# Spectral filter and two MLPs in float32 on one core: eight instead of four early products of the second sequence's first stage, and a reordered last group

## The chip, the core and the metric

The kernel runs on one core of a Trainium2 chip. The metric is the device time of one execution in microseconds (us), the whole program from the first to the last instruction and what little lies around it. TensorE multiplies matrices into PSUM, ScalarE (ACT) and VectorE (DVE) evacuate PSUM and do the elementwise work, GpSimd (POOL) does a few elementwise steps out of SBUF and issues some loads, and SyncE (SP) issues most of the DMA transfers.

## The reference, cut to what matters

```python
# batch 2, seq 3008, dim 256; d_ff 2048
X = np.fft.rfft(x, axis=1)
Y = X * (filt_r + 1j * filt_i)[None]
x = np.fft.irfft(Y, n=3008, axis=1).reshape(6016, 256)
h = x @ w_in                                   # first network
x = np.where(h > 0, h, np.exp(np.minimum(h, 0)) - 1) @ w_out
h = x @ w2_in                                  # second network
out = (h * np.clip(h + 3, 0, 6) / 6) @ w2_out
```
The inputs and weights are float32, or float64 where setup yields that; the output is float32.

## The kernel before, in words

**The transform.** A length of 3008 is 47 x 64. A sequence goes through four matrix stages: a first stage over 47 (table `s1` or `s1t`), a second over 64 (`s2`), the filter, the inverse second stage (`i2`), and the inverse first stage (`i1`). The dim of 256 is two halves h of 128. For sequence 0 all of this is the **prologue**; for sequence 1 it is done beside the first network's units. A string `PROLOGUE` is the order of the prologue, written out by hand. Its steps, with h and an index behind the letter, are:

- T: four transposes of first-stage results `zt`, and their copy out of PSUM; A: a first-stage piece of the second half (matmuls with `s1t`, then a copy into `zt`).
- S: the second-stage matmul and `mult`, three VectorE multiplications (L192 twice, L193) with the filter tile; GpSimd adds their results (L195). F: GpSimd flips the sign of part of the next filter tile (`f_sign`, L128). I: the inverse second-stage matmul (L200), its evacuation and a write to DRAM (L207).
- V: four reloads of these writes (L211), which wait for all six writes of a half. O and o: the inverse first stage (L219) with evacuation on ScalarE or VectorE. X: split of a block of the result for the first network.
- x: load of a tile of sequence 1 (`x_load`, SP); b: split of half such a tile into two float32r parts (ScalarE rounds, L78; VectorE subtracts, L79); B: the product of the first stage of sequence 1 on it, three matmuls (L82 to L84), its evacuation and write. M: split of the table `s1`; m: its load.
- w: load of a float64 weight tile as raw words (`w_raw`); c and k: steps of its conversion to two float32r parts (L261 to L286; c for weight tile 0).

`LOADS` is the order of the first loads on SP's queue: four tiles of sequence 0 (half 0), then F (filter tile), W (weight tile), X (tile of sequence 0, half 1).

**The first network** runs in 192 units of 12 matmuls, each a block of 512 tokens times a weight tile of 128 of d_ff: six for `g1`, six for `g2`. Lists `pre[n]` and `post[n]` hold what else is done at unit n: conversions of weights, and sequence 1's transform from unit 48 on (`s1(h, i, t)` puts a first-stage product at unit t, with its load, split and evacuation around it).

**The second network** runs over six pairs of blocks p and eight pairs of weight tiles q, 48 groups, with Strassen-like sums: seven products `prod(p, q, m)` of three matmuls and eight second products. A group's blocks (0,0), (1,1), (1,0), (0,1) each go through an add, `relu`, `gate` and `part` (ScalarE rounds, VectorE subtracts), then `second`. The blocks (1,0) and (0,1) of a group are finished in the next one, where it is `old`. `beside` holds work for the next pair: loads, four GpSimd subtractions (`x_sums`) and seven operand splits (`x_part`).

All products in float32 accuracy are three float32r matmuls (`mm3`): high times low, low times high, high times high. Buffers come from rotating pools: `wpool` of sixteen 4 KB tiles a partition for converted weights, `p4` and `p2` of twenty tiles.

## Time and profile before

| | |
|---|---|
| times of three runs | 1125.74, 1136.16, 2869.24 us (median 1136.16) |
| the profiled execution | 1131.49 us, span 1129.7 us |
| mean granted TensorE clock | 0.993 |
| TensorE busy | 1110.8 us, 98% of the span |
| VectorE, ScalarE, GpSimd busy | 884.0, 793.5 and 150.5 us |
| DMA in the first 84 us | 282, 299 and 254 GB/s in three stretches of 28 us |

TensorE is busy nearly throughout, and the chain of work that ended last lies on it for 90% of the span. That share says nothing of the first 76 us, in which the engines hand each other short pieces, nor of the last 13. [...] In a row of the timeline the bracket at the end is the idle time before it and what ended it.

### The profile page before, as it was taken

Reading aid. Unit: us, or ns where it says so; the run is one execution under the profiler, and the core shown is the slowest. Engines: PE = TensorE matmul, PEld = TensorE weight load, DVE = VectorE, ACT = ScalarE, POOL = GpSimd, SP = SyncE. Lnnn points to the kernel's source line nnn. Section 1 sums busy time; section 2 is a strip of 40 time slices with the busy share of each in tenths; the row PEclk is TensorE's granted clock in tenths of the full one; section 3 lists DMA queues with packets and bytes.
Section 4 is the critical chain, followed back from the end, with each engine's and each line's share of the span. In section 5 each row is a group of like instructions: output and inputs, shape, how many; then the busy total and the mean of one; then the engine's idle time right before and its main releaser. Section 6 shows DMA issues by size and latency. Waiting matters only on the chain.

```text
span 1129.7 us, 14294 instructions
## 1 busy us (share of the span) xinstructions
PE 1110.8 (98%) x5068; PEld 919.7 (81%) x5068; DVE 884.0 (78%) x1376; ACT 793.5 (70%) x1406; POOL 150.5 (13%) x141
## 2 busy tenths in 40 slices
PE   8899999999999999999999999999999999999997
PEld 5588888788789888888889878878878878888996
DVE  6979999669983588888897677777777777777775
ACT  3477777877766777777777667767767767767664
POOL 3600000013330011111224110010010010000000
PEclk9989999999999999999999999999999999999999
DMA  9973100364523123323427900200200200200100
GB/s 284 300 254 125 38 5 1 112 182 161 173 86 84 54 75 112 112 94 112 149 90 256 323 1 1 75 1 1 75 1 1 75 1 1 70 1 1 38 1 33
DMA packets 56472, 100.50 MB, mean 89 GB/s; under 512 B 4816, under 2 KB 33872, under 8 KB 56400
## 3 DMA queue, kind: packets, MB, share of 16 engines
q1 hardware_dynamic: 51968, 86.65, 23.2%
q0 software_dynamic: 3456, 12.58, 3.2%
q8 instruction: 40, 0.66, 0.2%
q10 hardware_dynamic: 976, 0.34, 0.1%
q14 instruction: 32, 0.26, 0.1%
HBM read 65.22 MB, written 34.34 MB: 88 GB/s over the span
## 4 chain that ended last, share of the span: by engine, by line
PE 90%; DVE 4%; DMA 2%; ACT 1%; issue 1%; POOL 0%; SPq 0%; ACTq 0%; DVEq 0%; POOLq 0%
PE ps L82 29%; PE ps L83 29%; PE ps L84 29%; PE ps L219 3%; DVE t L79 1%; DMA t<-in_fq 1%; DMA t<-in_xp 1%; DVE t L500 1%; PE ps L200 1%; DVE t L192 1%; DMA id<-in_ident 0%; DVE t L389 0%; DVE t L193 0%; DVE t L492 0%; POOL t L195 0%
## 5 line engine op out<-in xcount | busy, mean ns | idle before, releaser
L82 PE MATMUL ps<-t,w 128*128 128x512 f32 (+1 forms) x1296 | 502.5, 388 | 2.8 <-DVE t L79 2.6
L83 PE MATMUL ps<-t,w 128*128 128x512 f32 (+1 forms) x1296 | 500.0, 386 | 0.0
L84 PE MATMUL ps<-t,w 128*128 128x512 f32 (+1 forms) x1296 | 499.8, 386 | 0.0
L79 DVE TENSOR_TENSOR t<-t,t 128x512 fp32r<-128x512 f32 (+2 forms) x490 | 350.7, 726 | 80.7 <-ACT t L78 75.2
L78 ACT ACTIVATE t<-t 128x512 fp32r<-128x512 f32 (+2 forms) x490 | 293.6, 614 | 97.4 <-DVE t L500 72.8
L82 PEld LDWEIGHTS ps<-t,w 128*128 128x128 f32 x1296 | 243.7, 188 | 53.1 <-DVE t L79 3.5
L84 PEld LDWEIGHTS ps<-t,w 128*128 128x128 f32 x1296 | 243.7, 188 | 45.7
L83 PEld LDWEIGHTS ps<-t,w 128*128 128x128 f32 x1296 | 243.8, 188 | 45.2
L389 DVE SCALAR_TENSOR_TENSOR t<-t,ps 128x512 f32<-128x512 f32 (+1 forms) x192 | 129.2, 673 | 89.6 <-ACT t L388 88.3
L387 ACT ACTIVATE t<-ps 128x512 f32<-128x512 f32 (+1 forms) x192 | 112.2, 584 | 95.9 <-PE ps L84 95.7
L500 DVE SCALAR_TENSOR_TENSOR t<-t,t 128x512 f32<-128x512 f32 (+1 forms) x144 | 102.5, 712 | 33.9 <-ACT t L496 33.5
L496 ACT ACTIVATE t<-t,three 128x512 f32<-128x512 f32 (+1 forms) x144 | 97.6, 709 | 44.3 <-DVE t L492 43.0
L388 ACT ACTIVATE t<-t 128x512 f32<-128x512 f32 (+1 forms) x192 | 119.7, 623 | 6.1
L486 ACT ACTIVATE t<-ps 128x512 f32<-128x512 f32 (+1 forms) x144 | 83.3, 578 | 24.4 <-PE ps L84 23.2
L492 DVE TENSOR_TENSOR t<-ps,t 128x512 f32<-128x512 f32 (+1 forms) x144 | 94.2, 672 | 4.8 <-PE ps L84 2.3
L435 POOL TENSOR_TENSOR t<-t,t 128x512 f32<-128x512 f32 (+1 forms) x18 | 25.4, 1411 | 287.2 <-PE ps L84 281.4
L128 POOL TENSOR_TENSOR t<-t,sg 128x512 f32<-128x512 f32 x24 | 30.4, 1271 | 195.1 <-DMA t<-in_fq 195.1
L82 PE MATMUL ps<-t,t 128*128 128x512 f32 (+1 forms) x120 | 46.8, 390 | 3.4 <-ACT t L486 3.4
L84 PE MATMUL ps<-t,t 128*128 128x512 f32 (+1 forms) x120 | 46.3, 386 | 0.0
L83 PE MATMUL ps<-t,t 128*128 128x512 f32 (+1 forms) x120 | 46.3, 386 | 0.0
L195 POOL TENSOR_TENSOR t<-t,t 128x512 f32<-128x512 f32 x24 | 34.1, 1420 | 74.3 <-DVE t L193 56.5
L500 DVE SCALAR_TENSOR_TENSOR t<-t,ps 128x512 f32<-128x512 f32 (+1 forms) x48 | 32.3, 674 | 11.9 <-ACT t L496 11.9
(79 smaller groups left out, 854.4 us busy)
## 6 DMA issues: line engine op xcount, KB each, us to landing
t<-in_fq SPq DMA_DIRECT2D x24, 512.0 KB, 6.5
scrw<-t SPq DMA_DIRECT2D x16, 512.0 KB, 2.8
w<-scrw POOLq DMA_DIRECT2D x16, 512.0 KB, 7.5
t<-in_xp SPq DMA_DIRECT2D x16, 384.0 KB, 5.6
scr<-t SPq DMA_DIRECT2D x24, 256.0 KB, 2.5
t<-scr SPq DMA_DIRECT2D x16, 384.0 KB, 5.0
scrx<-t SPq DMA_DIRECT2D x10, 512.0 KB, 3.1
t<-scrx SPq DMA_DIRECT2D x10, 512.0 KB, 5.3
```

What stands on the lines that cost most here:

```text
L78: nc.scalar.activation(hi, src, AF.Copy)
L79: nc.vector.tensor_tensor(out=lo, in0=src, in1=_f32(hi), op=ALU.subtract)
L82: nc.tensor.matmul(acc, wh, xl, start=start, stop=False, skip_group_check=more)
L83: nc.tensor.matmul(acc, wl, xh, start=False, stop=False, skip_group_check=more)
L84: nc.tensor.matmul(acc, wh, xh, start=False, stop=stop, skip_group_check=more)
L387: nc.scalar.activation(r[:, :n], acc[:, :n], AF.Relu, scale=-1.0)
L388: nc.scalar.activation(r[:, :n], r[:, :n], AF.Exp, scale=-1.0)
L389: nc.vector.scalar_tensor_tensor(out=r[:, :n], in0=r[:, :n], scalar=-1.0, in1=acc[:, :n], op0=ALU.add, op1=ALU.max)
L486: nc.scalar.activation(t[:, : self.n], bank_[:, : self.n], AF.Copy)
L492: nc.vector.tensor_tensor(out=self.h[key][:, :n], in0=bank_[:, :n], in1=u[:, :n], op=ALU.add)
L496: nc.scalar.activation(self.g[key][:, : self.n], self.h[key][:, : self.n], AF.Relu, bias=three)
L500: nc.vector.scalar_tensor_tensor(out=r[:, :n], in0=r[:, :n], scalar=6.0, in1=self.h.pop(key)[:, :n], op0=ALU.min, op1=ALU.mult)
```

## The change

- The prologue's tail does eight instead of four first-stage products of sequence 1 (B00 to B07, all of half 0); `s1(0, 4..7)` at units 48 to 51 goes. All four x tiles are loaded in the prologue; the last two lie in two tiles of `wpool`.
- `LOADS` no longer holds W1 and W2, which the steps w00 and w01 load again anyway; W0 goes behind F10, F03 ahead of the X tiles.
- The conversion steps of weight tile 0 and the split of `s1` go behind the multiplications S10 to S15; `s1` is loaded at the start with the other tables.
- The zero-fill of x tiles beyond row 96 goes, and the first stage contracts 96 rows.
- In a group of the second network `old.part((0, 1))` goes behind the product 6 and its copy `u2`. The work for the next pair is spread: one GpSimd subtraction in each of the groups 1 to 4 instead of two in groups 2 and 3, loads one group earlier, splits from group 2.
- In the last group the two halves of `part` (`high`, `low`) are placed singly, ahead of the add that waits for product 3 where they can be, and the last evacuation is halved between ScalarE and VectorE.

```diff
     def x_load(b, h, q):
-        xin[b, h, q] = t4([P, 8, P])
-        if b == 0:
-            nc.vector.memset(xin[b, h, q][KP:], 0.0)
+
+        xin[b, h, q] = wpool.tile([P, 8, P], F32, tag="w", name=name("w")) if (b, h) == (1, 0) and q > 1 else t4([P, 8, P])
...
-    def out_evac(p, k):
+    def out_evac(p, k, last=False):
...
+            m = n if d == 0 else n // 2 if last else 0
+            if m:
+                nc.scalar.activation(t[:, :m], o[:, :m], AF.Copy, scale=1.0 / 6.0)
+            if m < n:
+                nc.vector.tensor_scalar_mul(t[:, m:n], o[:, m:n], 1.0 / 6.0)
...
+        def high(self, key):
+            g, gh = self.g[key], t2([P, 512], F32R)
+            nc.scalar.activation(gh[:, : self.n], g[:, : self.n], AF.Copy)
+            self.g[key] = g, gh
+
+        def low(self, key):
+            (g, gh), gl, n = self.g[key], t2([P, 512], F32R), self.n
+            nc.vector.tensor_tensor(out=gl[:, :n], in0=g[:, :n], in1=_f32(gh[:, :n]), op=ALU.subtract)
             self.g[key] = gh, gl
...
         g.relu((0, 0))
-        if old:
-            old.part((0, 1))
         g.gate((0, 0))
         prod(p, q, 6, a, False)
         u2 = g.copy(a)
+        if old:
+            old.part((0, 1))
...
-        A12 A13 c01 A14 I03 F01 c01 A15 A16 I04 c02 T10 T11 F01 I05 V00 T12 S10 x00 x01 T13 S11 T14 S12 M00 F01
-        T15 S13 I10 F01 S14 c01 I11 S15 I12 w00 O00 I13 b00 O01 c01 b01 I14 o02 I15 b02 c01 V10 w01 c01 b03 O03 X00
-        o04 X01 k02 O05 o06 X02 k02 B00 B01 B02 B03
+        A12 A13 A14 I03 F01 A15 A16 I04 T10 T11 F01 I05 c02 V00 T12 S10 x00 x01 x02 x03 T13 S11 T14 S12 F01
+        T15 S13 I10 F01 S14 I11 S15 I12 w00 O00 I13 c01 b00 O01 I14 c01 b01 o02 I15 M00 c01 b02 V10 w01 c01 b03 O03
+        X00 c01 o04 X01 k01 O05 B00 b04 o06 X02 b05 B01 B02 b06 k01 B03 B04 b07 k02 B05 B06 B07
...
-    for x in "F00 W0 F01 F02 X0 X1 X2 X3 F03 F04 W1 F05 F10 F11 F12 W2 F13 F14 F15".split():
+    for x in "F00 F01 F02 F03 X0 X1 X2 X3 F04 F05 F10 W0 F11 F12 F13 F14 F15".split():
...
-    for i in range(4, 8):
-        s1(0, i, T - 4 + i)
...
-            1: [(x2_load, 0), (x2_load, 1)], 2: [(x_sums, 0), (x_sums, 1)], 3: [(x_sums, 2), (x_sums, 3)],
-            4: [(x_part, 1), (x_part, 2)], 5: [(x_part, 6), (x_part, 5)], 6: [(x_part, 7), (x_part, 4)],
-            7: [(x_part, 3)],
+            0: [(x2_load, 0), (x2_load, 1)], 1: [(x_sums, 0)], 2: [(x_sums, 1), (x_part, 1)],
+            3: [(x_sums, 2), (x_part, 2)], 4: [(x_sums, 3), (x_part, 5)], 5: [(x_part, 6)],
+            6: [(x_part, 7), (x_part, 4)], 7: [(x_part, 3)],
...
         prod(5, NF // 2 - 1, 3, old.c, False)
+        old.high((1, 1))
+        old.gate((1, 0))
         old.add((0, 1), old.u2, old.c)
+        old.low((1, 1))
+        old.high((1, 0))
         old.relu((0, 1))
-        old.part((1, 1))
-        old.gate((1, 0))
+        old.low((1, 0))
         old.gate((0, 1))
-        old.part((0, 1))
-        old.part((1, 0))
-        old.second((0, 0))
-        old.second((1, 1))
-        old.second((0, 1))
-        out_evac(old.p, 1)
-        old.second((1, 0))
-        out_evac(old.p, 0)
+        old.high((0, 1))
+        old.low((0, 1))
+        for key in ((0, 0), (1, 1), (1, 0), (0, 1)):
+            old.second(key)
+            if key == (1, 0):
+                out_evac(old.p, 0)
+        out_evac(old.p, 1, True)
```

First place: VectorE in the prologue, from the second to last copy into `zt` to the first multiplication of the second half (S10). `raw_132` and `raw_150` are weight tile 0's raw words, `t_93` and `t_88` the copy of T11's transposes. Before:

```order
L75 COPY zt_328<-ps_365 128x5x4x24
L262 TENSOR_SCALAR t_81_373<-raw_132 128x512
L266 SCALAR_TENSOR_TENSOR t_81_373<-raw_132,t_81_373 128x512
L75 COPY zt_328<-ps_391 128x5x4x24
L268 SCALAR_TENSOR_TENSOR t_80_372<-t_80_372,t_81_373 128x512
L270 TENSOR_SCALAR t_81_373<-t_80_372 128x512
L75 COPY t_93_421<-ps_416 128x512
L192 TENSOR_TENSOR t_104_447<-ps_444,t_18_160 64x512 x2
```

and in the changed kernel:

```order
L75 COPY zt_314<-ps_351 128x5x4x24
L75 COPY zt_314<-ps_371 128x5x4x24
L75 COPY t_88_399<-ps_394 128x512
L261 TENSOR_SCALAR t_92_408<-raw_150 128x512
L265 SCALAR_TENSOR_TENSOR t_92_408<-raw_150,t_92_408 128x512
L191 TENSOR_TENSOR t_102_431<-ps_428,t_16_148 64x512 x2
```

The four conversion steps stood ahead of T11's copy, two of them ahead of the last `zt` copy; now two stand behind that copy, and the other two behind S15.

Second place: VectorE in the last stages of the prologue, from the split of the second block (X01) to the last conversion step there. `t_174` and `t_183` or `t_187` are blocks of the result, `raw_545` and `raw_528` weight tile 1, `w_441` and `w_443` the two x tiles in the weight pool. Before:

```order
L79 TENSOR_TENSOR t_174_643<-t_148_572,t_173_642 128x512
L262 TENSOR_SCALAR t_177_650<-raw_545 128x512
L266 SCALAR_TENSOR_TENSOR t_177_650<-raw_545,t_177_650 128x512
L75 COPY t_180_662<-ps_664 128x188
L79 TENSOR_TENSOR t_183_669<-t_155_593,t_182_668 128x512
L268 SCALAR_TENSOR_TENSOR t_176_649<-t_176_649,t_177_650 128x512
L270 TENSOR_SCALAR t_177_650<-t_176_649 128x512
```

and in the changed kernel:

```order
L79 TENSOR_TENSOR t_174_633<-t_148_556,t_173_632 128x512
L261 TENSOR_SCALAR t_177_640<-raw_528 128x512
L79 TENSOR_TENSOR t_184_660<-w_441,t_183_659 96x512
L75 COPY t_180_651<-ps_663 128x188
L79 TENSOR_TENSOR t_187_668<-t_154_575,t_186_667 128x512
L79 TENSOR_TENSOR t_189_672<-w_441,t_188_671 96x512
L79 TENSOR_TENSOR t_194_688<-w_443,t_193_687 96x512
L265 SCALAR_TENSOR_TENSOR t_177_640<-raw_528,t_177_640 128x512
L79 TENSOR_TENSOR t_199_705<-w_443,t_198_704 96x512
L267 SCALAR_TENSOR_TENSOR t_176_639<-t_176_639,t_177_640 128x512
L269 TENSOR_SCALAR t_177_640<-t_176_639 128x512
```

Four subtractions for the added products (b04 to b07) have come in between, the last of them two steps ahead of the end.

Third place: ScalarE at the head of a group of the second network. The two copies out of one `ps` are those after product 1 and after product 6 (`u2`); the rows with `three` are the `relu` of (0,1) and (0,0), and the rounding of (0,1) reads the first of these. Before:

```order
L486 ACTIVATE t_1554_6636<-ps_6630 128x512
L78 ACTIVATE t_1556_6643<-t_1547_6615 128x512
L496 ACTIVATE t_1558_6647<-t_1550_6628,three 128x512
L496 ACTIVATE t_1559_6656<-t_1555_6641,three 128x512
L78 ACTIVATE t_1560_6658<-t_1558_6647 128x512
L486 ACTIVATE t_1562_6666<-ps_6630 128x512
L78 ACTIVATE t_1563_6671<-t_1559_6656 128x512
```

and in the changed kernel:

```order
L487 ACTIVATE t_1553_6625<-ps_6619 128x512
L78 ACTIVATE t_1555_6632<-t_1546_6604 128x512
L497 ACTIVATE t_1557_6636<-t_1549_6617,three 128x512
L497 ACTIVATE t_1558_6645<-t_1554_6630,three 128x512
L487 ACTIVATE t_1559_6651<-ps_6619 128x512
L78 ACTIVATE t_1560_6653<-t_1557_6636 128x512
L78 ACTIVATE t_1562_6660<-t_1558_6645 128x512
```

The copy `u2` has moved ahead of the rounding of (0,1), which reads what VectorE's gate writes.

## Rows read from the trace of the kernel before

**Rows 1.** Busy time by stretch, after the prologue: us, engines' busy (instructions), clock, DMA.

```profile
197.00:1129.70 932.70, 922.53 (x4174) 771.91 (x4172) 713.13 (x1099) 664.65 (x1176) 120.74 (x112) 1.00 0.23 77
```

**Rows 2.** Timeline of TensorE in the prologue: start, us, instruction, idle time before it.

```profile
38.01 1.06 PE L152 MATMUL ps<-id,zt 128*128 128x128 f32 x8 [2.54 <-DVE zt L75]
...
52.79 1.63 PE L200 MATMUL ps<-t,i 128*128 128x512 f32 x2 [1.42 <-POOL t L195]
...
54.21 2.29 PE L219 MATMUL ps<-i,t 96*128 96x94 f32 x10
...
69.22 7.28 PE L219 MATMUL ps<-i,t 96*128 96x94 f32 x64
```

**Rows 3.** Busy time by stretch, behind that wait; clock and DMA share near the end.

```profile
56.00:60.00 4.00, 4.00 (x15) 2.97 (x15) 2.55 (x4) 2.25 (x5) 1.58 (x1) 0.50 0.50 167
```

**Rows 4.** Second network: TensorE's wait in all, then timelines of GpSimd, VectorE, ScalarE.

```profile
PE ps L82 <- ACT t L486: 3.4, 5, 0.7
...
661.00 1.30 POOL L435 TENSOR_TENSOR t<-t 128x512 f32<-128x512 f32 x1 [8.94 <-ACT t L486]
662.26 1.74 POOL L435 TENSOR_TENSOR t<-t,t 128x512 f32<-128x512 f32 x1
...
661.64 1.20 DVE L79 TENSOR_TENSOR t<-t,t 128x512 fp32r<-128x512 f32 x1
662.77 1.77 DVE L500 SCALAR_TENSOR_TENSOR t<-t,t 128x512 f32<-128x512 f32 x1
...
665.85 0.68 DVE L500 SCALAR_TENSOR_TENSOR t<-t,t 128x512 f32<-128x512 f32 x1
...
664.58 0.63 ACT L78 ACTIVATE t<-t 128x512 fp32r<-128x512 f32 x1 [1.95 <-DVE t L500]
```

**Rows 5.** The tail: timelines of VectorE and TensorE, and busy time by stretch.

```profile
1117.10 0.62 DVE L492 TENSOR_TENSOR t<-ps,t 128x448 f32<-128x448 f32 x1 [1.08 <-PE ps L84]
...
1119.61 0.47 PE L82 MATMUL ps<-t,w 128*128 128x448 f32 x1 [1.33 <-DVE t L79]
...
1122.01 0.74 PE L82 MATMUL ps<-t,w 128*128 128x448 f32 x1 [0.89 <-DVE t L79]
...
1121.00:1125.00 4.00, 3.11 (x9) 2.69 (x9) 1.51 (x3) 1.30 (x3) 0.00 (x0) 0.58 0.00 0
```

**Rows 6.** Timeline of VectorE in the prologue, and busy time by stretch (VectorE's is third).

```profile
26.41 1.39 DVE L192 TENSOR_TENSOR t<-ps,t 64x512 f32<-64x512 f32 x2 [2.42 <-POOL t L128]
...
34.58 0.94 DVE L262 TENSOR_SCALAR t<-raw 128x512 uint32<-128x512 uint32 x1
35.56 1.41 DVE L266 SCALAR_TENSOR_TENSOR t<-raw,t 128x512 uint32<-128x512 uint32 x1
...
47.84 1.37 DVE L102 TENSOR_TENSOR s_l<-s,s_h 128x96 fp32r<-128x96 f32 x1
...
53.38 0.90 DVE L272 SCALAR_TENSOR_TENSOR t<-raw,t 128x512 f32<-128x512 uint32 x1
...
41.32:56.39 15.07, 13.35 (x51) 7.66 (x49) 14.72 (x22) 5.25 (x9) 8.75 (x7) 0.90 0.91 250
56.39:70.04 13.65, 13.65 (x69) 10.76 (x69) 9.50 (x18) 8.41 (x18) 1.58 (x1) 0.74 0.51 150
```

**Rows 7.** Timeline of TensorE in the main loop: two matmuls twelve apart.

```profile
92.26 0.39 PE L84 MATMUL ps<-t,w 128*128 128x512 f32 x1
...
94.98 0.39 PE L84 MATMUL ps<-t,w 128*128 128x512 f32 x1
```

**Rows 8.** Timelines of GpSimd and of SP's DMA issues in the prologue.

```profile
25.34 1.04 POOL L128 TENSOR_TENSOR t<-t,sg 128x512 f32<-128x512 f32 x1 [2.25 <-DMA t<-in_fq]
...
19.17 5.32 SPq L123 DMA_DIRECT2D t<-in_fq  x4
...
43.04 1.73 SPq L211 DMA_DIRECT2D t<-scr  x4
...
65.20 1.73 SPq L211 DMA_DIRECT2D t<-scr  x4
```

More of the change, by code (lines that the diff above doesn't have):

```diff
@@ L139, in s1t @@
             nc.tensor.matmul(
-                acc[:, (j - j0) * KP : (j - j0 + 1) * KP], xin[b, h, j // 8][:, j % 8, :],
-                mats["s1t"], start=True, stop=True,
+                acc[:, (j - j0) * KP : (j - j0 + 1) * KP], xin[b, h, j // 8][:KP, j % 8, :],
+                mats["s1t"][:KP], start=True, stop=True,
             )
@@ L472, in out_evac @@
             o, t = outs.pop((p, k, d)), t2([P, 512])
-            if d == 0:
-                nc.scalar.activation(t[:, :n], o[:, :n], AF.Copy, scale=1.0 / 6.0)
-            else:
-                nc.vector.tensor_scalar_mul(t[:, :n], o[:, :n], 1.0 / 6.0)
+            m = n if d == 0 else n // 2 if last else 0
[3 more added lines that the diff above has]
+                nc.vector.tensor_scalar_mul(t[:, m:n], o[:, m:n], 1.0 / 6.0)
             nc.sync.dma_start(out[d * P : (d + 1) * P, t0 : t0 + n], t[:, :n])
@@ L508, in part @@
             self.g[key] = gh, gl
+        def high(self, key):
[5 more added lines that the diff above has]
+            nc.vector.tensor_tensor(out=gl[:, :n], in0=g[:, :n], in1=_f32(gh[:, :n]), op=ALU.subtract)
+            self.g[key] = gh, gl
         def second(self, key, d=(0, 1)):
@@ L606, in fft_conv_moe_moe2 @@
     PROLOGUE = """
-        T00 T01 T02 S00 T03 F01 S01 T04 F01 S02 T05 F01 S03 I00 F01 S04 I01 F01 m00 A10 A11 S05 I02 F01
-        A12 A13 c01 A14 I03 F01 c01 A15 A16 I04 c02 T10 T11 F01 I05 V00 T12 S10 x00 x01 T13 S11 T14 S12 M00 F01
-        T15 S13 I10 F01 S14 c01 I11 S15 I12 w00 O00 I13 b00 O01 c01 b01 I14 o02 I15 b02 c01 V10 w01 c01 b03 O03 X00
-        o04 X01 k02 O05 o06 X02 k02 B00 B01 B02 B03
+        T00 T01 T02 S00 T03 F01 S01 T04 F01 S02 T05 F01 S03 I00 F01 S04 I01 F01 A10 A11 S05 I02 F01
+        A12 A13 A14 I03 F01 A15 A16 I04 T10 T11 F01 I05 c02 V00 T12 S10 x00 x01 x02 x03 T13 S11 T14 S12 F01
+        T15 S13 I10 F01 S14 I11 S15 I12 w00 O00 I13 c01 b00 O01 I14 c01 b01 o02 I15 M00 c01 b02 V10 w01 c01 b03 O03
+        X00 c01 o04 X01 k01 O05 B00 b04 o06 X02 b05 B01 B02 b06 k01 B03 B04 b07 k02 B05 B06 B07
         O10 o11 X10 O12 X11 k03 O13 X12 O14 O15 O16
@@ L704, in fft_conv_moe_moe2 @@
     with tc.manual_schedule():
-        for key, src in (("s1t", cs1t), ("id", ident), ("sg", sg), ("s2", cs2), ("i2", ci2), ("i1", ci1)):
+        for key, src in (("s1t", cs1t), ("id", ident), ("sg", sg), ("s2", cs2), ("i2", ci2), ("i1", ci1), ("s1", cs1)):
             load_mat(key, src)
@@ L768, in fft_conv_moe_moe2 @@
                 s1_evac(1, h, g)
-            elif what == "m":
-                load_mat("s1", cs1)
             elif what == "M":
```

## The prediction

> **What bounds the kernel now.** I began with the page's totals and then asked where TensorE idles: after the prologue it is busy for 922.53 of 932.70 us [rows 1]. So there an edit is worth either the matmul time that it takes off TensorE or the holes that it closes, about 10 us of them in all. Next I listed TensorE's waits by cause and looked up each in the timeline. [...] In the second network five holes stand behind ScalarE's copy L486, 3.4 us together [rows 4]. At the end two holes of 1.33 and 0.89 us stand behind the last group's subtractions, and the clock is 0.58 on the mean from 1121 to 1125 [rows 5]. The prologue itself is a chain on VectorE, which works for 14.72 of the 15.07 us from 41.32 to 56.39 [rows 6].
>
> **The sum is made against the profiled execution:** 1131.49 us, of which the span is 1129.7. It lies between the two ordinary runs shown (1125.74 and 1136.16, mean 1130.95). The third, 2869.24, is no ordinary run, so the median of the three is simply the slower ordinary one.
>
> **Term A, the four products that leave the main loop.** Each is three matmuls of 512 columns, so twelve. Two matmuls twelve apart start at 92.26 and 94.98 [rows 7]: 2.72 us. They stood at units 48 to 51, in the stretch where TensorE hardly idles [rows 1], so all of it is on the path: -2.7.
>
> **Term B, the holes in the second network.** At 661.00 and 662.26 two GpSimd subtractions run back to back, and VectorE's gate L500 beside the second takes 1.77 us instead of 0.68. ScalarE idles 1.95 us for that gate, with its rounding L78 of block (0,1) at the head of its queue; the copy L486 that TensorE needs for product 7 stands behind it, and TensorE loses 0.7 [rows 4]. The change takes the cause away twice: the copy goes ahead of that rounding (third place of the order), and a group holds one GpSimd subtraction, never two. The five holes go: -3.4. What is late next in a group is the rounding and subtraction of (0,1), about 0.6 + 0.7 us, which TensorE wants only after products 5 and 7 and two pairs of second products: 18 matmuls, 4.1 us by [rows 7]. So nothing follows. [...]
>
> **Term C, the tail.** In the last group TensorE finishes six second products after product 3, then waits 1.33 and later 0.89 us [rows 5], because every rounding and subtraction follows the add that waits for product 3 (1117.10 to 1117.72). In the new order the rounding of (1,1) and the gate of (1,0) go ahead of that add. At 0.6 us a piece, from the add's end: subtraction (1,1) until 1118.4, (1,0) until 1118.9, last gate 1119.5, rounding 1120.1, subtraction (0,1) 1120.7. TensorE's blocks of six matmuls of 448 columns (1.2 us, by columns from [rows 7]) want them at 1118.2, 1119.4 and 1120.6, so 0.3 of the 2.2 us of holes stay. With the holes I expect the low clock to stay away. [...] The last evacuation, a VectorE instruction as long as that add (0.62 us), is cut into halves on two engines: -0.3. Sum -(1.9 + 1.6 + 0.3) = -3.8; the bound is -2.2 if the clock falls all the same.
>
> **Term D, the prologue,** along VectorE.
> - The multiplication S03 begins at 26.41 after 2.42 us of waiting [rows 6] for the filter tile F03, whose sign GpSimd makes once the load is there, at 25.34 [rows 8]. F03 is now loaded ahead of the four X tiles, and F04 takes the queue place that F03 had, since W0 went behind. So S04 can follow one GpSimd instruction after 25.34, at 26.4 instead of 28.6: -2.2 for all behind it.
> - The word steps L262 and L266, 0.94 + 1.41 us, stood ahead of the last zt copy [rows 6] and go behind T11's copy (first place of the order). The transposes at 38.01 then start at about 33.5. S10 has those two steps in front of it, but no longer the next two and no idle time: about 38.4 instead of 41.32, -2.9.
> - Of the 15.07 us from there to the end of S15, the split of s1 (0.2 + 1.37) and L272 (0.90) leave [rows 6]: 12.6. S15 ends at about 51.0, -5.4.
> - Then the bill. From 56.39 to 70.04 VectorE works 9.50 us and idles 4.1 [rows 6]. Behind S15 now come also L268 and L270 (1.1), the split (about 1.2), L272 (0.7) and four subtractions for the added products (0.65 each): 15.1 without a hole, so 66.1 instead of 70.04 (second place of the order). The last subtraction for a product stands two steps ahead of that, at 65.2; as ScalarE's roundings ahead of it are queued with evacuations, I take 66.0.
> - TensorE does not bind here: from about 54 it has 34 small rows (3.9 us by the 64 in 7.28 [rows 2]) and 24 matmuls (5.5 us). B07 ends at 66.7 and O10 starts there instead of 69.22: -2.5. The 64 rows behind it take 7.1 us as before (their last one's end overlaps the next), and the main loop starts at 73.8 instead of 76.3.
> - O10 also needs the reload V1, issued at 65.20 [rows 8] and there within 4.0 us, since O10 started at 69.22 without a wait. The transfers that begin with the reload V0 at 43.04 fill the DMA engines until they are half idle in 56 to 60 [rows 3, 8]. They begin 4 us earlier now and hold two x tiles of 384 KB more. Four tiles of 512 KB were issued in 5.32 us with the queue full [rows 8], 1.33 each, so two of 384 KB are 2.0 to 2.7: they end at about 57, the last writes behind them at 58 to 59, and V1 is there by 63. That is 3 us of cover; if the -2.9 did not come, it would be gone.
> So D is -2.5; its bounds are -5.5 (ScalarE and VectorE keep pace with TensorE, B07 at 63.7) and +2.6 (the clock, first rival).
>
> **At nothing:** the eight zero-fills on VectorE, because what TensorE waits for next is the fourth x load and a later ScalarE copy; 96 instead of 128 rows contracted, since time goes by columns; the second loads of W1 and W2, whose places in the queue are in D; the early load of s1, behind six other small ones; the two x tiles in two of sixteen weight buffers, read out by 67, long before the fifteenth weight tile wants one.
>
> Sum: -2.7 - 3.4 - 3.8 - 2.5 = -12.4, so 1131.49 - 12.4 = **1119 us**.
>
> **Rivals.** *The clock falls again, later.* In my working TensorE waits for the operands of B04 to B07, 2.8 us of work in about 6. Before, the drop followed a hole of 1.42. If it drops again, it falls on the 64 rows of O1x and the first units: a spell of 10 us, as before, costs up to 5.1, and D turns from -2.5 to +2.6: 1124. For it: the same kind of hole, longer. Against: the wait of 2.54 at 38 brought no drop. [...] *The products only change place.* TensorE has no hole from 54 to 76, so one may say that eight products there cost what four in the loop cost, and D is -2.5 + 2.7, nothing: 1121.5. [...] *GpSimd's delay spreads.* Two delays, 1.20 - 0.68 and 1.77 - 0.68, are 1.6 us and cost TensorE 0.7, so 0.9 was free; a full subtraction of 1.30 [rows 4] would cost 0.4, in 20 groups 8 us, and B is +8 instead of -3.4: 1130. Against: the copy no longer stands behind the gate. *Slower:* VectorE's subtraction for (0,1) now waits for a rounding that waits for the copy after product 6, in 47 groups, with the subtraction of (0,0), the operand splits and the next add queued behind it. If TensorE then waits d in each group, the time is 1119 + 47 d: from d = 0.27 it is slower than before, and with a full subtraction of 0.69 it is 1151. Against: the 4.1 us of cover, and that the gate of (0,0) now goes ahead.
>
> **How the numbers follow.** Forecast 0.50, clock 0.23, products only moved 0.15, GpSimd 0.04, slower 0.02; 0.06 for a better case, in which the clock does not fall in the prologue or the tail (the ordinary runs lie 10.4 apart, twice the price of such a spell): 1125.74 - 12.4 = 1113. The range takes in that case, the first two rivals and, above 1124, half the spread of the runs: 1112 to 1129. Two per cent, about what a measurement of this kernel can tell from no change, is 23 us, twice my sum. So within 2%: 0.93; faster by more 0.05, where the better case is set against the slower ordinary run; slower by more 0.02.
>
> **What would show it.** A: twelve matmuls fewer in units 48 to 51. B: no wait of TensorE for the copy in the second network, though gates beside GpSimd are still long. C: TensorE's last 24 matmuls without a hole over 0.4 us, at full clock. D: the second half's transposes at 33 to 34, S15's end near 51, O10 near 66.7, the first unit near 73.8, the granted clock at 1.00 there. I would be wrong if the clock shows a spell behind B04, if O10 waits for V1, or if TensorE has a new short wait in each group.

## The result

The changed kernel is about 1% slower. It takes 1142.5 us (median of four runs, 1139.7 to 1145.2) against 1132.6 for the kernel before, a ratio of 1.0108 with a 95% interval of 1.0071 to 1.0146. One of the four runs of the kernel before took 2869.24 us and is left out of the ratio, which rests on the other three (1125.74 to 1136.16). The forecast was 1119, its range 1112 to 1129. The profiled execution took 1143.72 us, 1142.0 of it the span.

First I cut the span at events that both kernels have: TensorE's first product of the main loop, and the first and the last matmul that reads the sums of the weights (zt) in the second network. These are the three stretches between and behind them, first in the kernel before, then in the changed one (us, engines' busy time with instructions, granted clock as a share of full speed, DMA share, GB/s).

```profile
76.28:633.02 556.74, 555.25 (x2536) 464.23 (x2536) 456.20 (x717) 422.26 (x771) 91.80 (x89) 1.00 0.35 117
633.02:1071.10 438.08, 434.68 (x1918) 358.74 (x1916) 333.33 (x514) 303.07 (x515) 28.94 (x23) 1.00 0.09 32
1071.10:1129.71 58.61, 52.78 (x251) 47.81 (x249) 36.40 (x63) 33.30 (x61) 0.00 (x0) 0.96 0.05 16
```

```profile
100.84:655.25 554.41, 552.90 (x2525) 463.04 (x2524) 450.74 (x708) 417.26 (x759) 91.81 (x89) 1.00 0.33 110
655.25:1086.74 431.49, 431.49 (x1917) 359.63 (x1916) 335.40 (x514) 301.65 (x515) 28.57 (x23) 1.00 0.09 32
1086.74:1141.95 55.21, 51.10 (x251) 46.70 (x249) 35.97 (x63) 33.22 (x62) 0.00 (x0) 0.99 0.05 18
```

Each stretch got shorter: by 2.3, 6.6 and 3.4 us. In the second network TensorE is now busy for 431.49 of 431.49 us, and near the end, where [rows 5] show holes and the lower clock, a window of the changed kernel has neither:

```profile
1133.00:1137.00 4.00, 3.93 (x20) 3.32 (x19) 2.91 (x6) 2.28 (x4) 0.00 (x0) 1.00 0.01 4
```

All of the loss lies ahead of the main loop, which starts at 100.84 us instead of 76.28; the forecast was 73.8. These are the rows of TensorE there, which answer to [rows 2] (start, us, instruction, idle time before it), first the start of the kernel before, then the changed kernel:

```profile
5.32 3.87 PE L139 MATMUL ps<-s1t,t 128*128 128x96 f32 x32 [0.22 <-DVE t L118]
10.43 3.78 PE L139 MATMUL ps<-s1t,t 128*128 128x96 f32 x32 [1.24 <-DMA t<-in_xp]
14.88 1.50 PE L152 MATMUL ps<-id,zt 128*128 128x128 f32 x12 [0.67 <-ACT zt L73]
...
17.16 0.60 PE L152 MATMUL ps<-id,zt 128*128 128x128 f32 x4
```

```profile
5.30 13.97 PE L138 MATMUL ps<-s1t,t 96*128 96x96 f32 x64 [0.20 <-DMA s1t<-in_cs1t]
19.85 2.82 PE L151 MATMUL ps<-id,zt 128*128 128x128 f32 x12 [0.58 <-ACT zt L73]
...
24.17 0.62 PE L151 MATMUL ps<-id,zt 128*128 128x128 f32 x4
...
81.33 0.71 PE L82 MATMUL ps<-t,s_h 96*96 96x512 f32 x1 [10.58 <-DVE t L79]
...
85.94 0.74 PE L82 MATMUL ps<-t,s_h 96*96 96x512 f32 x1 [3.05 <-DVE t L79]
...
87.34 13.80 PE L218 MATMUL ps<-i,t 96*128 96x94 f32 x64
```

Three things are new. The 64 first rows (32 products: the trace counts a float32 matmul as two) take 13.97 us without a stop, where they took 3.87 and 3.78, so the first transposes start 5.0 us later; these still run at half speed (2.82 us for 1.50), and the next group starts 7.0 us later (24.17 for 17.16). TensorE waits 10.58 and 3.05 us for operands of the added products B06 and B07. Behind that the 64 rows that read the last reload take 13.80 us where they took 7.28 [rows 2]. The windows of the two idle times and of what follows show the clock, which answers to [rows 3]:

```profile
71.00:81.30 10.30, 0.00 (x0) 0.00 (x1) 0.81 (x2) 1.59 (x3) 0.00 (x0) 0.55 0.72 221
81.30:102.00 20.70, 17.62 (x73) 16.14 (x74) 8.43 (x15) 8.60 (x20) 0.00 (x0) 0.50 0.58 178
```

While TensorE stood idle for 10.30 us, the granted clock fell to its lower level (0.55 on the mean), and it stayed there until the main loop had begun (0.50 from 81.30 to 102.00 us). TensorE's wait is put down to VectorE's subtraction, but VectorE works 0.81 us in 10.30. So the next step is what VectorE waits for, and it is ScalarE: first ScalarE's waits for these writes (us in all, times, longest), then its timeline, then SyncE's DMA issues.

```profile
ACT t L168 <- DMA scr<-t: 16.9, 3, 10.7
...
68.07 0.59 ACT L168 ACTIVATE t<-ps 96x512 f32<-96x512 f32 x1
79.35 0.59 ACT L168 ACTIVATE t<-ps 96x512 f32<-96x512 f32 x1 [10.69 <-DMA scr<-t]
79.84 0.62 ACT L78 ACTIVATE t<-w 96x512 fp32r<-96x512 f32 x1
...
67.29 1.73 SPq L210 DMA_DIRECT2D t<-scr  x4
...
71.59 18.57 SPq L170 DMA_DIRECT2D scr<-t  x4
```

L168 evacuates an added product, and two of them fill one tile, which L170 writes to DRAM. The next pair's evacuation takes the slot of the tile that is being written, so it waits until that write has landed. The rounding L78 of the next operand is queued behind it on ScalarE; VectorE's subtraction needs that rounding, and TensorE needs the subtraction. The first write was issued at 71.59, behind the reload of the second half and four loads of weights, and took 7.7 us to land; the other three took about 3 us, and the evacuations that wait for them 3.1 us each.

### The profile page after: what moved, and what is told of

Same layout as the page of the kernel before. It is cut to its first block, busy times and chain, and to the rows that moved or that the text cites. A ratio compares the mean times of both kernels' runs of the same rounds, so it can differ in the third digit from the quotient of the medians.

```text
span 1142.0 us, 14236 instructions
## 1 busy us (share of the span) xinstructions
PE 1118.4 (98%) x5068; PEld 931.6 (82%) x5068; DVE 875.8 (77%) x1368; ACT 792.6 (69%) x1407; POOL 148.6 (13%) x141
## 4 chain that ended last, share of the span: by engine, by line
PE 91%; DMA 4%; DVE 2%; ACT 1%; issue 1%; POOL 1%; SPq 0%; ACTq 0%; POOLq 0%
PE ps L82 29%; PE ps L84 29%; PE ps L83 29%; PE ps L218 2%; DMA t<-in_fq 2%; DMA scr<-t 1%; DMA t<-in_xp 1%; DVE t L79 1%; PE ps L138 1%; PE ps L199 1%; POOL t L194 0%; DMA id<-in_ident 0%; DVE t L388 0%; PE ps L182 0%; ACT t L78 0%
## 5 line engine op out<-in xcount | busy, mean ns | idle before, releaser
L79 DVE TENSOR_TENSOR t<-t,t 128x512 fp32r<-128x512 f32 (+2 forms) x483 | 343.8, 731 | 30.0 <-ACT t L78 27.5
L78 ACT ACTIVATE t<-t 128x512 fp32r<-128x512 f32 (+2 forms) x483 | 285.1, 613 | 30.1 <-POOL t L194 23.9
L83 PEld LDWEIGHTS ps<-t,w 128*128 128x128 f32 x1296 | 243.6, 188 | 45.2
L501 DVE SCALAR_TENSOR_TENSOR t<-t,t 128x512 f32<-128x512 f32 (+1 forms) x144 | 98.8, 712 | 33.6 <-ACT t L497 33.4
L493 DVE TENSOR_TENSOR t<-ps,t 128x512 f32<-128x512 f32 (+1 forms) x144 | 97.0, 678 | 25.3 <-ACT t L487 20.4
L497 ACT ACTIVATE t<-ps,three 128x512 f32<-128x512 f32 (+1 forms) x48 | 32.6, 680 | 28.6 <-PE ps L84 28.6
```

Source lines behind the costliest of these rows:

```text
L78: nc.scalar.activation(hi, src, AF.Copy)
L79: nc.vector.tensor_tensor(out=lo, in0=src, in1=_f32(hi), op=ALU.subtract)
L83: nc.tensor.matmul(acc, wl, xh, start=False, stop=False, skip_group_check=more)
L493: nc.vector.tensor_tensor(out=self.h[key][:, :n], in0=bank_[:, :n], in1=u[:, :n], op=ALU.add)
L497: nc.scalar.activation(self.g[key][:, : self.n], self.h[key][:, : self.n], AF.Relu, bias=three)
L501: nc.vector.scalar_tensor_tensor(out=r[:, :n], in0=r[:, :n], scalar=6.0, in1=self.h.pop(key)[:, :n], op0=ALU.min, op1=ALU.mult)
```

## Experiments

Ratios are to the kernel before, whose median was 1130.1 to 1132.6 us from one series to the next, so runs of different series are compared by ratio. Two theories were to be told apart from rivals: that the write's landing is what stalls the stage, and that the 96 contracted rows are what slowed its start.

**128 rows again.**

```diff
+        if b == 0:
+            nc.vector.memset(xin[b, h, q][KP:], 0.0)
...
-                ... xin[b, h, j // 8][:KP, j % 8, :], mats["s1t"][:KP], ...
+                ... xin[b, h, j // 8][:, j % 8, :], mats["s1t"], ...
```

> The changed kernel with the zero-filled rows and the full 128-row contraction of its first stage put back; all else stays. Theory (fewer contracted rows leave TensorE at its lower clock from the start until about 23 us): the 64 first products take about 7.7 us as before instead of 13.97, the first transposes stand near 15 instead of 19.85 us, every later step of the stage before the main loop comes about 5 us sooner, and the time falls from 1142.5 to about 1137.5 us. Rival (the late start comes from the order of the loads): the first transposes stay at 19 to 20 us and the time stays at 1142 to 1143 us. The two waits for TensorE behind the evacuations (10.6 and 3.1 us) stay in either case.

Measured: 1140.3 us, 1.0081 [1.0055, 1.0108]. The start answers to the theory, the total less so:

```profile
5.36 5.83 PE L140 MATMUL ps<-s1t,t 128*128 128x96 f32 x48 [0.36 <-DVE t L119]
12.93 2.00 PE L140 MATMUL ps<-s1t,t 128*128 128x96 f32 x16 [1.75 <-DMA t<-in_xp]
15.64 1.50 PE L153 MATMUL ps<-id,zt 128*128 128x128 f32 x12 [0.72 <-DVE zt L75]
...
83.00 13.80 PE L220 MATMUL ps<-i,t 96*128 96x94 f32 x64
```

The transposes come 4.2 us earlier, the next group 6.2 (17.92 for 24.17), and the last reload's products 4.3, because TensorE now waits longer: 2.12 us instead of 0.71 for B04's operand, and 11.15 instead of 10.58 for B06's. The wait for B07's stays at 3.05. The spans differ by 3.5 us and the medians by 2.2, but the intervals of the two ratios overlap, so what the rows cost is read from the trace here and not from the times.

**Own tiles for the evacuated pairs** (three in the idle zt buffer, one new):

```diff
         if jq % 2 == 0:
-            s1o[h] = t4([KP, 2, 512])
+            if h == 0 and jq == 0:
+                own["z"] = p12.tile([P, 3, 2, 512], F32, tag="zt", name=name("zt"))
+                own["c"] = const.tile([P, 2, 512], F32, name="own")
+            if h == 0:
+                s1o[h] = own["c"][:KP] if jq == 6 else own["z"][:KP, jq // 2]
+            else:
+                s1o[h] = t4([KP, 2, 512])
```

> The changed kernel with a tile of its own for each of the four pairs of evacuated products of the second sequence, so that no evacuation waits for the write of the pair before it; the writes stay where they are on SyncE's queue. Theory (the evacuations wait for their write, the splits are queued behind them on ScalarE, and the clock falls because TensorE then idles): the idle times of 10.6 and 3.1 us go, the granted clock stays at 1.00 through the last reload's products, these take 7.3 instead of 13.8 us, the main loop starts near 80 instead of 100.8 us, and the time is about 1122 us. Rival A (VectorE cannot take the subtractions at this pace): the idle time stays for the most part, now behind VectorE's own work, and the time stays above 1135 us. Rival B (the clock falls there whatever the idle time): only 13.6 us are won, the last reload's products still take 13.8 us, and the time is about 1129 us.

Measured: 1122.1 us, 0.9920 [0.9892, 0.9947], as the theory had it. No evacuation waits for a write, TensorE's waits there are 1.0 us at most, and in the profiled run the clock does not fall (1.00 in every stretch from 56 to 110 us):

```profile
5.28 13.97 PE L138 MATMUL ps<-s1t,t 96*128 96x96 f32 x64 [0.18 <-DMA s1t<-in_cs1t]
...
73.22 7.28 PE L224 MATMUL ps<-i,t 96*128 96x94 f32 x64
```

Rivals A and B fall in this run. Three of the eight runs had a mean clock of 0.989 to 0.991 and took 1124.4 to 1126.3 us, the others 0.998 and more and 1116.6 to 1122.3; the three have no trace, so whether their clock fell amid the short waits that are left is not shown. By the medians the one wait and what hung on it cost 20 us.

**Both edits together.**

> The two edits above together: 128 contracted rows in the first stage, and own tiles for the evacuated products. If both theories hold and add up: about 1117 us, that is 5 us under the kernel with own tiles alone, with the main loop starting near 75 us. If the rows cost nothing: the same time as with own tiles alone.

Measured: 1125.2 us, 0.9947 [0.9924, 0.9971]: not 5 us under the kernel with own tiles, but 3 over it, whose median mixes runs of both clocks. The start is early (transposes at 14.69) and so are the last reload's products, yet they run at the lower clock:

```profile
66.38 13.80 PE L226 MATMUL ps<-i,t 96*128 96x94 f32 x64
...
60.00:64.00 4.00, 2.63 (x10) 1.17 (x9) 3.70 (x8) 4.00 (x9) 0.00 (x0) 1.00 0.63 178
64.00:84.00 20.00, 19.74 (x80) 17.79 (x79) 7.99 (x15) 9.06 (x21) 0.00 (x0) 0.50 1.06 360
```

TensorE waited 0.72, 0.56 and 0.26 us for subtractions there; the kernel with own tiles alone has the same kind of waits (1.01, 0.56, 0.49) at full clock. One of the ten runs of this kernel had a mean clock of 1.00 and took 1115.3; the other nine had 0.99 and 1124 to 1128. So this is the prediction's first rival, the clock that falls again, and whether it falls changes from run to run.

**The writes on another queue.**

```diff
-            nc.sync.dma_start(
+            (nc.sync if h else nc.gpsimd).dma_start(
                 scr1[b][h][:, (jq - 1) * 512 : (jq + 1) * 512], flat(s1o.pop(h))
```

> The changed kernel with the four writes of the second sequence's evacuated products issued by GpSimd instead of SyncE; the tiles are reused as in the changed kernel, so each evacuation still waits for the write of the pair before it. Theory (the write is late because it is queued behind the reloads and the weights' loads on SyncE): the write lands some 2 to 4 us after its evacuation, the waits of 10.7 and 3.1 us shrink to under 3 us each, the clock stays up, and the time is 1122 to 1128 us. Rival (the write is late because the transfers themselves are slow, or the slot is held by something else): the waits stay and the time stays near 1142 us.

Measured: 1142.0 us, 1.0085 [1.0060, 1.0111]. My theory of SyncE's queue falls. GpSimd issued the first write at once, and it still took over 8 us to land (GpSimd's issue, then ScalarE's evacuation):

```profile
69.17 0.70 POOL L170 DMA_DIRECT2D scr<-t  x1 [9.28 <-ACT t L168]
...
77.67 0.59 ACT L168 ACTIVATE t<-ps 96x512 f32<-96x512 f32 x1 [8.81 <-DMA scr<-t]
```

In this kernel and in the changed one the DMA engines are busy throughout from 70 to 75 us (share 1.01, 269 and 270 GB/s), whichever engine issued the write. Issuing it on GpSimd gave 1.6 us less idle time on TensorE (8.96 for 10.58) and no less time in total.

**The reload behind the products,** so that its 1.57 MB are not ahead of the write.

```diff
-        ... c01 b02 V10 w01 c01 b03 O03 ...
+        ... c01 b02 w01 c01 b03 O03 ...
-        ... B05 B06 B07
+        ... B05 B06 B07 V10
```

> The changed kernel with the reload of the second half (1.57 MB in four transfers) issued behind all eight products of the second sequence instead of ahead of the first; the tiles are reused as in the changed kernel. If the write was slow because the reload's bytes went ahead of it on the shared DMA engines: the second pair's evacuation waits under 4 us instead of 10.7, the eight products end before 75 us, and then the products of the last stage wait for the reload until about 83 us; the time is 1128 to 1136 us. If a write takes its 8 us whatever is ahead of it: the waits of 10.7 and 3.1 us stay, the reload comes on top, and the time is 1145 us or more.

Measured: 1133.7 us, 1.0003 [0.9978, 1.0028], inside the range that I gave for the first theory. The products follow each other, B07 at 68.41, and TensorE then waits for the reload. The clock is low here as well: it fell before that wait (B07's three matmuls take 0.74, 0.63 and 0.63 us, B04's 0.45, 0.40 and 0.39), and the 64 rows take 13.94 us (TensorE, then ScalarE's evacuation of B02 and SyncE's issue of the writes):

```profile
68.41 0.74 PE L82 MATMUL ps<-t,s_h 96*96 96x512 f32 x1 [0.29 <-DVE t L79]
76.56 13.94 PE L218 MATMUL ps<-i,t 96*128 96x94 f32 x64 [6.56 <-DMA t<-scr]
...
65.03 0.60 ACT L168 ACTIVATE t<-ps 96x512 f32<-96x512 f32 x1
...
65.17 5.80 SPq L170 DMA_DIRECT2D scr<-t  x4
```

The run tests less than I meant it to. The writes land within 3.0 to 3.3 us, the first no longer in 7.7, so the bytes ahead did make it slow. But the waits did not go for that reason alone: the second pair's evacuation starts at 65.03, before the first pair's write is issued, so it has another slot, and the tiles are not reused as in the changed kernel. The reload's four tiles come out of the same pool of twenty and are taken later here; that they left the pairs one slot in the changed kernel is my reading of the code, which no run tests alone. What a write of 3 us costs with the slot shared is seen in the changed kernel's later pairs, 3.1 us of waiting each.

**The waits filled.** The changed kernel, with products of zeros in the two long idle times.

```diff
+                acc = bank() if g in (5, 6) else None
+                for _ in range({5: 10, 6: 3}.get(g, 0)):
+                    nc.tensor.matmul(acc, warm[:, :P], warm, start=True, stop=True)
                 s1_evac(1, h, g)
```

> The changed kernel, its waits for the writes left as they are, with 13 extra products of 128x512 zeros (used nowhere) in TensorE's two long waits, ten and three. Theory (the clock falls because TensorE idles, and this is a cost of its own beside the 13.6 us of waiting): the clock stays at 1.00, the evacuations' waits stay 10.7 and 3.1 us, the last 64 products take 7.3 instead of 13.8 us, the main loop starts near 94 instead of 100.8 us, and the time is about 1135 us. Rival (the clock's fall is not from this idle time): 0.50 from about 71 us as before, the extra products take some 2 us each or 26 us together, and the time is 1150 us or more.

Measured: 1133.5 us, 1.0037 [1.0015, 1.0060]. The waits are the same and the clock is back:

```profile
77.11 0.59 ACT L168 ACTIVATE t<-ps 96x512 f32<-96x512 f32 x1 [10.75 <-DMA scr<-t]
...
84.72 7.28 PE L218 MATMUL ps<-i,t 96*128 96x94 f32 x64
...
91.79 0.48 PE L82 MATMUL ps<-t,w 128*128 128x512 f32 x1
```

From that evacuation to the main loop it takes 14.7 us (77.11 to 91.79) where the changed kernel takes 21.5 (79.35 to 100.84): 6.8 us are the clock. Of the 20 us that own tiles took away these 6.8 are the clock's fall, and the rest is waiting. (Another 2.2 us of this run are an earlier start.)

**Short waits filled too:** both edits, and five products of 256 columns of zeros where TensorE waits for subtractions.

```diff
+                if g in (0, 3, 4, 5, 6):
+                    nc.tensor.matmul(bank()[:, :256], warm[:, :P], warm[:, :256], start=True, stop=True)
```

> The kernel with 128 contracted rows and own tiles, and five extra products of 128x256 zeros (their results are used nowhere) behind the first, fourth, fifth, sixth and seventh of the second sequence's products, where TensorE waits for VectorE. Theory (the clock falls there because TensorE is idle in these waits): the clock stays at 1.00 up to the main loop, the last reload's 64 products take 7.3 instead of 13.8 us, and the time is about 1116 us, as in the one run of the kernel without them whose clock was 1.00 throughout. Rival (the fall does not come from these waits): the granted clock is still 0.50 from about 64 us on, and the time is 1125 us or a little more.

Measured: 1117.1 us, 0.9854 [0.9820, 0.9888], mean clocks of 0.997 and more in all six runs. It is faster than both kernels.

```profile
14.24 1.50 PE L153 MATMUL ps<-id,zt 128*128 128x128 f32 x12 [0.72 <-DVE zt L75]
...
34.08 1.06 PE L153 MATMUL ps<-id,zt 128*128 128x128 f32 x8
...
65.15 7.28 PE L226 MATMUL ps<-i,t 96*128 96x94 f32 x64
```

**Only the second network and the last group** of the change, on the kernel before.

> The kernel before with only the last two parts of the change: the new order of the subtractions and loads in the second network, and the new last group. Terms B and C of the prediction: 3.4 + 3.8 us less than before, so about 1123.5 us against 1130.6. Rival (what VectorE's and ScalarE's queues give there is taken back by other waits): within 2 us of the kernel before.

Measured: 1119.0 us, 0.9873 [0.9837, 0.9910]: 13 us less, nearly twice the forecast. The stretches of its profiled run (1127.7 us, with a spell of the lower clock in its prologue, where ten rows of L219 take 2.29 us at 55.48 and 1.25 at 51.64):

```profile
639.45:1070.95 431.50, 431.50 (x1918) 359.63 (x1917) 335.41 (x514) 302.01 (x515) 28.54 (x23) 1.00 0.09 32
1070.95:1125.93 54.98, 51.09 (x251) 46.68 (x249) 35.97 (x63) 33.25 (x62) 0.00 (x0) 1.00 0.05 18
```

6.6 and 3.6 us, so 10.2 are the two parts. The other 3 are not traced to code that differs: six of the seven runs had a mean clock of 0.998 or more, against four of 23 of the kernel before.

**Four products instead of eight,** in the kernel with the short waits filled.

```diff
-        ... O05 B00 b04 o06 X02 b05 B01 B02 b06 k01 B03 B04 b07 k02 B05 B06 B07
+        ... O05 B00 o06 X02 B01 B02 k01 B03 k02
...
+    for i in range(4, 8):
+        s1(0, i, T - 4 + i)
```

> The filled kernel (128 rows, own tiles, extra products) with only the first four of the second sequence's products in the first sequence's last stages, the other four back in the main loop as before (four extra products of zeros in place of five). Term A of the prediction: four products of three matmuls come back on the path at full load, and the main loop is 2.7 us longer, against a stage ahead of it that is shorter by what the four cost there: if they were free there, 1119.8 us; if they only change place (the rival at 15 in 100), 1117 us, the same time.

Measured: 1115.9 us, 0.9863 [0.9844, 0.9882], the rival's figure. The main loop with four products is first, that with eight second:

```profile
69.17:625.89 556.72, 555.23 (x2536) 464.24 (x2536) 455.21 (x716) 421.66 (x769) 92.77 (x89) 1.00 0.35 116
```

```profile
72.21:625.74 553.53, 551.96 (x2524) 462.44 (x2524) 452.53 (x712) 418.16 (x761) 92.45 (x89) 1.00 0.35 115
```

The loop is 3.2 us shorter with eight, and starts 3.0 us later (72.21 for 69.17). Both kernels carry the extra products, which leave TensorE hardly a hole in that stage; how much of four more products the holes would take in without them is shown only by the one run of 1115.3 us with both edits, at full clock, which took as long as four products do.

**96 rows elsewhere.** The kernel before with 96 rows, and the filled kernel with 96 rows; the edit is the first experiment's, turned round.

> The kernel before with one edit: its first stage contracts 96 rows, and the zero-fills of the other 32 go. If fewer rows keep TensorE at its lower clock from the start: the 64 first products take about 14 us instead of some 8, the first transposes stand near 19.5 instead of 14.9 us, and the time goes up by about 5 us, to some 1135 us. If rows don't matter, and only the order of loads and the other parts of the change made the changed kernel's start late: the first transposes stay near 15 us and the time is that of the kernel before, within 2 us.

> The filled kernel (own tiles, five extra products) with 96 instead of 128 contracted rows in the first stage and without the zero-fills. If fewer rows are what keeps the clock low at the start: in most runs the first transposes stand near 19.8 us and the time is about 1121 to 1122 us, 5 above that of the filled kernel with 128 rows (1117.1). If the start's clock falls out one way or the other whatever the rows: the times are those of the kernel with 128 rows, 1117 us, within 1.5.

Measured: 1131.8 us, 0.9994 [0.9966, 1.0021], and 1118.7 us, 0.9891 [0.9871, 0.9911]. The theory as I had put it fails in the first: this start ran at full clock with 96 rows. The second bears out neither expectation: its profiled run, the slowest at 1122.1, has the slow start, and the other five took 1116.1 to 1120.0, neither mostly 1121 to 1122 nor all near 1117. (First the run of the kernel before, then the filled kernel.)

```profile
5.16 4.36 PE L137 MATMUL ps<-s1t,t 96*128 96x96 f32 x32
10.26 3.81 PE L137 MATMUL ps<-s1t,t 96*128 96x96 f32 x32 [0.74 <-DMA t<-in_xp]
```

```profile
5.45 13.97 PE L138 MATMUL ps<-s1t,t 96*128 96x96 f32 x64 [0.35 <-DMA s1t<-in_cs1t]
...
80.06 0.48 PE L82 MATMUL ps<-t,w 128*128 128x512 f32 x1
```

The slow start puts the main loop of the filled kernel at 80.06 instead of 72.21, and the span of the profiled run at 1120.3 instead of 1112.5. So where no long wait hides part of it, it costs 7.8 us and not 5.

Of the seven profiles with 96 rows four have the 13.97. Two more (the reload moved, the waits filled) began at full clock, dropped to the lower level around a wait of 0.92 and 2.07 us for a load, and ran the first transposes at half speed, 2.82 us. Of the six profiles so far with 128 rows none has either. But one of them, the last two parts alone, also began at half speed: its 64 rows took 9.81 us, with six or seven in a window of one microsecond until about 10 us, as in the changed kernel's start, and twelve from 11 us on (eleven in the kernel before; rows on an edge count in both windows).

```profile
5.58 9.81 PE L139 MATMUL ps<-s1t,t 128*128 128x96 f32 x64 [0.48 <-DMA s1t<-in_cs1t]
```

**Rows alone,** in trains behind the last output.

```diff
+        for k in range(12):
+            rows = (P, KP)[k % 2]
+            for _ in range(40):
+                nc.vector.memset(flat(xw), 0.37)
+            acc = bank()
+            for _ in range(192):
+                nc.tensor.matmul(acc[:, :KP], flat(xw)[:rows, :P], flat(xw)[:rows, P : P + KP], start=True, stop=True)
```

> The kernel of the four-product run, and behind its last output twelve trains of 192 products of the first stage's size (96 columns each, of a constant, used nowhere), the odd trains contracting 128 rows and the even ones 96, each after a pause in which TensorE is idle while VectorE rewrites the operand 40 times. Its time is only that of the added work; what is read is the granted clock in each train. If fewer rows keep the clock low: the trains of 128 rows reach 1.00 within some 7 us and take about 26 us, the trains of 96 rows stay at 0.50 for 18 us or for the whole train, up to 42 us. If rows don't matter: trains of both kinds rise alike, and their lengths differ by less than 2 us.

Measured (2455 us in all): the six trains of 128 rows take 45.2 to 46.3 us, the six of 96 rows 82.2. The first two, with TensorE's granted clock ahead of the DMA share:

```profile
1159.05:1204.20 45.15, 45.15 (x384) 44.98 (x384) 0.00 (x0) 0.00 (x0) 0.00 (x0) 0.95 0.00 1
1251.92:1334.15 82.23, 82.23 (x384) 81.99 (x384) 0.00 (x0) 0.00 (x0) 0.00 (x0) 0.50 0.00 1
```

TensorE is busy throughout in both, and both begin at the lower level (the first train has 0.64 in its first 6 us and 1.00 in the next 5). From there a train of 96 rows never rose.

## Why the prediction was wrong

**The step of term D that failed** is the bill of VectorE and the sentence "as ScalarE's roundings ahead of it are queued with evacuations, I take 66.0". I took the evacuations as work on ScalarE and did not ask what their tile waits for. From the second pair on each pair's first evacuation waits for the write of the pair before, and the first of these writes comes behind the reload and the weights on the DMA engines. The seventh and eighth operands are queued behind the first two of these waits, 10.69 and 3.11 us, and the last subtraction for a product starts at 85.20 us where I had it end at 65.2. In the kernel before no operand stood behind an evacuation: its four were made before the first one. Own tiles take 20 us away, and the filled waits show that 6.8 of the 20 are the clock. That the bytes ahead made the first write slow is shown by its landing (7.7 us, and 3.0 to 3.3 with the reload behind).

**The step "96 instead of 128 rows contracted, since time goes by columns", at nothing,** failed too. At full clock the count of rows cost nothing here: twenty rows of the first stage's second half take 2.37 us in the kernel before and in the changed one. But the changed kernel's start stayed at the lower level for some 18 us by its durations (13.97 us for the 64 rows, 2.82 for the first transposes), and in the trains of 96 rows the clock stayed at 0.50 from idle for all of 82.2 us. In the kernel's own start, which four rows of products of zeros with 128 contracted rows precede, the outcome changes from run to run. So the price is nothing in some runs and up to 7.8 us in others.

**The rest of term D held.** With both out of the way, in the filled kernel, S04's multiplications start at 25.74 (forecast 26.4), the transposes of the second half at 34.08 (33.5), S10's at 37.39 (38.4), the last reload's products at 65.15 (66.7), and the main loop at 72.21 (73.8).

**Term A** was the second rival: the products only change place. The loop is shorter by 3.2 us at full clock (2.3 in the changed kernel, whose loop begins at the lower level), and the stage ahead longer by 3.0. That part of the stretch ran at a granted clock of 0.50 in the kernel before [rows 3] has nothing to say against that rival once the stretch runs at full clock.

**Term B** had the right place and was too small: -6.6 instead of -3.4. TensorE has no wait for the copy left, though the longest gate still takes 1.78 us (1.77 before), as I had said would show it. The list of waits gave 3.4 [rows 4], but TensorE's busy time fell by 3.2 as well (434.68 to 431.49) for the same matmuls. The starts show most of that: in the kernel before the five holes cost 4.2 us from start to start, and fifteen other matmuls start 0.26 to 0.38 us behind the one before them instead of 0.23, another 1.6; the changed kernel has neither. Which of the two remedies did it, the copy's place or the spread subtractions, was not taken apart. **Term C** held, -3.4 for -3.8, and TensorE has no listed wait left in the tail. No run shows by itself the 1.6 us that the sum of C puts on the clock: what the runs show is the whole stretch, 58.61 us at a granted clock of 0.96 in the kernel before, 55.21 at 0.99 in the changed one and 54.98 at 1.00 with the last two parts alone.

**The rivals.** The first came, in another form: the clock did fall behind B04, but behind a wait of 10.58 us that I had not seen, and it cost 6.5 us on the 64 rows where I had put 5.1 in all, half of the spell of the kernel before. That spell, behind TensorE's wait of 1.42 us for GpSimd [rows 2]:

```profile
53.30:63.50 10.20, 10.20 (x34) 7.56 (x33) 6.09 (x11) 4.72 (x10) 3.69 (x3) 0.50 0.57 179
```

The third and fourth did not come: the second network got 6.6 us shorter, and TensorE is busy for all of its 431.49 us.

The pieces of the profiled run: the main loop at 100.84 for 73.8 is +27.0; A, B and C together are 2.3 + 6.6 + 3.4 = 12.3 for 9.9, -2.4; so 1119.0 + 24.6 = 1143.6, and it took 1143.72. (This adds up what was measured, and tests nothing.) Of the 27.0, the two long waits are 13.6, the clock on the 64 rows 6.5, and the slow start 7.0 by the second group of transposes. That these make 27.1 is partly chance: short waits of 0.71 and 0.56 us are left out, and the filled kernel came 1.6 us ahead of the forecast.

What stays open: what left the added pairs one slot in the pool, why the clock falls behind short waits in the kernel with both edits (profiled run 0.50 from 64 to 84 us, a mean of 0.99 in nine runs of ten) and not behind waits of the same kind in that with own tiles alone (profiled run 1.00), why a start with 96 rows runs at full speed in one run and not in the next, and why the kernel with the last two parts alone had fewer such spells in an unchanged prologue.

## What to carry to other kernels

When work goes into a stage, follow the tiles of every instruction that it adds to the event that sets them free: here an evacuation whose slot waited 10.69 us for a DRAM write held up all that was queued behind it on ScalarE, and the write was late with the reload and the weights ahead of it, whichever engine issued it (7.7 us by SyncE, over 8 by GpSimd, 3.0 to 3.3 with the reload behind). Work that leaves a full stretch is a gain only where the stretch that takes it has holes (here 3.2 us came off the loop and 3.0 went on ahead of it); compare the two stretches at the same clock. Take the pieces of a change apart before judging the whole: here two parts alone were worth 13 us by the medians, 10 by their own stretches, and the prologue's part lost more than that.

## What the runs showed of the hardware

- Trains of matmuls that contract 96 rows took 82.2 us, six times of six, with TensorE busy throughout (granted clock 0.50 over the whole of the first two), where the starts of the kernels with 96 rows sometimes ran at full speed (4.36 and 3.81 us for 64 rows); trains of 128 rows of the same columns took 45.2 to 46.3 us (0.95 and 0.93 in the first two). (The operand was a constant.)
- The clock column reads 1.00 in the first slices of the changed kernel, where the first 64 rows take 13.97 us and the transposes 2.82 instead of 1.50: there the durations, not that column, show the level.
- In the second network the list of TensorE's waits showed half of what their cause cost: 3.4 us were listed, 6.6 came back. The time from one matmul's start to the next showed more of it, 5.8 us.
